# A 2x2x3 block product in 11 products instead of 12 for the last group's hidden layer, and the last x transposed two pieces later

## The chip, the cores and the metric

The kernel runs on one core of a Trainium2 chip. The metric is the device time of one execution in microseconds (us). PE is TensorE, DVE is VectorE, ACT is ScalarE, POOL is GpSimd, SP is SyncE. SBUF is the core's working memory; PSUM is the memory that matmuls write, eight banks of 512 fp32 values per partition. All arithmetic is in fp32.

## The reference

Two blocks follow each other. A delta-rule attention runs over 4 batches of 8 heads, 768 positions and 48 dimensions, and its output, 3072 tokens by 384, goes into a feed-forward layer with three first-layer weights and a maximum:

```python
for t in range(S):
    y[:, :, t] = np.einsum('bhd,bhde->bhe', q[:, :, t], state)
    v_old = np.einsum('bhde,bhd->bhe', state, kt)
    state = state + bt * np.einsum('bhd,bhe->bhde', kt, vt - v_old)
x = y.transpose(0, 2, 1, 3).reshape(3072, 384)
h = np.maximum(np.maximum(x @ w1, x @ w2), x @ w3)      # 3072 x 768
out = h @ w_out                                          # 3072 x 384
```

Here kt is the normalized key. The changed code belongs to `x @ w` for the last 512 tokens.

## The kernel before

The attention is worked in chunks of 64 positions, and the tokens go through the feed-forward layer in `GROUPS` = 6 groups of 512. The order of the instructions is written out by hand. The generator `ffn(m)` yields after each piece of the feed-forward work of group m; the loop at L1319 runs over these pieces, numbered from 0, and after each one issues the links of the attention of the next group that `LINKS` (L1210) names for that piece. So group m's matmuls lie between the attention steps of group m + 1. Within an engine, instructions run in the order in which they are issued.

`hidden(f, lo, w)` (L1050) makes one tile of 128 features of h for 512 tokens, feature-major. `less_first` has replaced w2 and w3 by w2 - w1 and w3 - w1, so that from group 1 on h is max(0, x(w2 - w1), x(w3 - w1)), and x w1 is added after the second layer as x (w1 w_out), whose matrix `both_layers` leaves in `w_sb[0]`. That leaves two weights, `w_sb[1]` and `w_sb[2]`. For each of the six feature tiles and each of the two weights, three matmuls of 128x128 by 128x512 (L1057) sum over the 384 inner values in a tile of `ps_ffn`, which has two buffers. ScalarE writes the first weight's product to h with a Relu (L1067); VectorE takes the maximum with the second's (L1071). This makes 12 pieces.

`outputs(m, hs)` (L947) makes the second layer of the last two groups, also with fewer block products (Winograd's form of Strassen's scheme, with weights that `cross_weights` prepares): 11 pieces of products of 192 columns (L960), with sums on VectorE (L989) and copies on ScalarE (L994, L1011, L1015, L1021). The pieces of group 4 (`GROUPS - 2`) are thus 0 to 11 for the hidden layer and 12 to 22 for the outputs. Group 5, the last, has no attention beside it.

The last x comes to the last group in two halves of 256 tokens: y is written to DRAM (`y_blocks`, L839), read back in another order (`read_y`, link w, L850) and transposed in blocks of 32 by VectorE (`turn_y`, link X, L861). Of group 5's halves, X0 stands after piece 14 of group 4 and X1 after piece 17. In VectorE's queue X1 thus stands behind the three differences issued in piece 17 (`op(s14[j], a12[j], s32[j], minus)`, L1023) and ahead of the sums of pieces 18 to 22.

`ps_two` (L83) gives PSUM tiles of two banks, three of them in turn. `kpad` and `kmore` are SBUF tiles that hold keys while the attention runs; `w_bits` is the tag of five SBUF buffers in which weights and turned keys are staged, and `square` that of 17 buffers for h, among others.

Of the kernel before, what the change touches and what calls it, by code (L numbers as in the profile page):

```python
# [9 lines left out]
FP32 = mybir.dt.float32  # L10
# [4 lines left out]
ALU = mybir.AluOpType  # L15
# [8 lines left out]
def kernel(  # L24
# [31 lines left out]
    nc = tc.nc  # L56
# [5 lines left out]
    KT = DM // 128  # L62
    FT = DFF // 128
    NP = H // 2
    UNITS = NCH * 2
    GROUPS = UNITS // 4
# [5 lines left out]
    work = ctx.enter_context(tc.tile_pool(name="work", bufs=2))  # L72
# [7 lines left out]
    def ps_ffn(shape, name):  # L80
        return psum.tile(shape, FP32, name=name, tag="ffn", bufs=2)

    def ps_two(name):  # L83
        return psum.tile([128, 2, 512], FP32, name=name, tag="two", bufs=3)


    kpad = [const.tile([128, H, DP], FP32, name=f"kpad{i}") for i in range(4)]
    kmore = [const.tile([128, 2, H, DP], FP32, name=f"kmore{i}") for i in range(2)]
# [20 lines left out]
    def rows(bb):  # L109
        return slice(C * bb, C * (bb + 1))  # L110
# [70 lines left out]
    for bb in range(2):  # L181
        nc.gpsimd.affine_select(
            out=mask[rows(bb)], in_=mask[rows(bb)], pattern=[[1, C]], base=-1,
# [4 lines left out]
    t1 = [const.tile([128, 2, H, BL], FP32, name=f"t1{i}") for i in range(NU)]  # L188
# [5 lines left out]
    w_sb = [const.tile([128, KT, DFF], FP32, name=f"w{i}_sb") for i in range(3)]  # L194
# [112 lines left out]
    def square(name):  # L307
        return work.tile([128, H, C], FP32, name=name, tag="square", bufs=17)
# [169 lines left out]
    def blocks(m, queue=nc.sync):  # L478
        if m == 1:
            xs[m] = in_wo(0)  # L480
        else:
            xs[m] = work.tile([128, 2, HB * BL + HB], FP32, name="x_bl", bufs=1)
        queue.dma_start(
            out=in_rows(xs[m]),
            in_=at_d[m].rearrange("c f b h j i -> (c f b h) j i"),
        )
# [232 lines left out]
    xts, rhss, qss, us, yts = {}, {}, {}, {}, {}  # L719
# [184 lines left out]
    PAIRS = FT // 2  # L904
    crossed = {}

    def cross_weights(part):

        left, right = slice(0, HALF), slice(HALF, DM)
        top, bottom = wo_sb[:, 0:PAIRS], wo_sb[:, PAIRS:FT]  # L910
        spare = w_sb[0][:, :, DM : 2 * DM]
        minus = nc.vector.tensor_tensor
        if part == 0:
            minus(
                out=spare[:, :, right], in0=bottom[:, :, right], in1=top[:, :, right],
                op=ALU.subtract,
            )
            minus(
                out=top[:, :, right], in0=top[:, :, right], in1=top[:, :, left],
                op=ALU.subtract,  # L920
            )
            return
        minus(
            out=spare[:, :, left], in0=bottom[:, :, right], in1=top[:, :, right],
            op=ALU.subtract,
        )
        fourth = []
        for n in range(2):
            t = work.tile([128, DM], FP32, name="mant", bufs=2)
            for i in range(2 - n):  # L930
                fourth.append(t[:, HALF * i : HALF * (i + 1)])
        for j in range(PAIRS):
            minus(
                out=fourth[j], in0=wo_sb[:, PAIRS + j, left], in1=spare[:, j, left],
                op=ALU.subtract,
            )
        crossed.update(
            b11=[top[:, j, left] for j in range(PAIRS)],
            b21=[bottom[:, j, left] for j in range(PAIRS)],
            b22=[bottom[:, j, right] for j in range(PAIRS)],  # L940
            t1=[top[:, j, right] for j in range(PAIRS)],
            t2=[spare[:, j, left] for j in range(PAIRS)],
            t3=[spare[:, j, right] for j in range(PAIRS)],
            t4=fourth,
        )

    def outputs(m, hs):  # L947
# [95 lines left out]
        store(m5, 1, 1)  # L1043
        yield

    def ffn(m):
        xt = xts[m]
        hs = {}

        def hidden(f, lo, w):  # L1050
            if f not in hs:
                hs[f] = square("h").rearrange("p h c -> p (h c)")
            h = hs[f][:, lo : lo + w]
            for i in range(m > 0, 3):
                p_h = ps_ffn([128, TOK], "p_h")[:, 0:w]
                for t in range(KT):
                    nc.tensor.matmul(  # L1057
                        p_h,
                        w_sb[i][:, t, f * 128 : (f + 1) * 128],
                        xt[:, t, lo : lo + w],  # L1060
                        start=(t == 0),
                        stop=(t == KT - 1),
                    )
                if i == 0:
                    nc.scalar.copy(h, p_h)
                elif m and i == 1:
                    nc.scalar.activation(  # L1067
                        out=h, in_=p_h, func=mybir.ActivationFunctionType.Relu
                    )
                else:  # L1070
                    nc.vector.tensor_tensor(out=h, in0=h, in1=p_h, op=ALU.max)  # L1071
                yield


        early = FT // 2 if m == 0 else 0
        for lo in (0, TOK // 2):
            for f in range(early):
                yield from hidden(f, lo, TOK // 2)
        for f in range(early, FT):
            yield from hidden(f, 0, TOK)  # L1080
        if m >= GROUPS - 2:
            yield from outputs(m, hs)
            return
        for i in range(4):
            cc, g = divmod(i, 2)
            p_o = ps_ffn([128, DM], "p_o")
            last = slice(i * 128, (i + 1) * 128)
            terms = [(hs[f][:, last], wo_sb[:, f]) for f in range(FT)]
            if m:
                terms += [(xt[:, t, last], w_sb[0][:, t, 0:DM]) for t in range(KT)]  # L1090
            for n, (stays, moves) in enumerate(terms):
                nc.tensor.matmul(  # L1092
                    p_o, stays, moves, start=(n == 0), stop=(n == len(terms) - 1)
                )
                if m and n == 4:
                    yield
            o_sb = work.tile([128, DM], FP32, name="o_sb")
            nc.scalar.copy(o_sb, p_o)  # L1098
            for bb in range(2):
                tok0 = (2 * bb + g) * S + (2 * m + cc) * C  # L1100
                nc.sync.dma_start(out=out[tok0 : tok0 + C, :], in_=o_sb[rows(bb)])
            yield
# [3 lines left out]
    def some(gen, n):  # L1106
        for _ in range(n):
            if next(gen, gen) is gen:
                break
# [74 lines left out]
    for _ in range(2):  # L1184
# [25 lines left out]
    LINKS = {  # L1210
# [3 lines left out]
    }  # L1214
    EARLY_LINKS = {
# [19 lines left out]
        t=turn, K=load_k, L=lambda n: load_blocks(n, nc.sync),  # L1235
# [4 lines left out]
    def links(m, names):  # L1240
        for name in names.split():
            f, i = name[0], int(name[1])
            if f in RECURS and m < GROUPS:
                RECURS[f](2 * m + i)
            elif f in MADE and m + 1 < GROUPS:
                MADE[f](2 * (m + 1) + i)
            elif f in UNIT and m + 1 < GROUPS:
                UNIT[f](4 * (m + 1) + i)
            elif f == "N" and m + 2 < GROUPS:
                load_blocks(4 * (m + 2) + i)  # L1250

    def queries(names):
        for name in names.split():
            f, n = name[0], int(name[1])
            if f not in OF_KEYS:
                links(0, name)
                continue
            OF_KEYS[f](n)
            if f == "T" and n + 3 < 11:
                load_q(n + 3)  # L1260
# [5 lines left out]
    for i, _ in enumerate(ffn(0)):  # L1266
# [15 lines left out]
        queries(FIRST.get(i, ""))  # L1282
        links(1, EARLY_LINKS.get(i, ""))
        if i == 20:
# [34 lines left out]
    for m in range(1, GROUPS):  # L1319
        for i, _ in enumerate(ffn(m)):  # L1320
            if i == 0:
                some(solving, 3)
            if m == 1 and i in (2, 5, 8):
                both_layers(i // 3)
            if m == GROUPS - 2 and i in (8, 9):
                cross_weights(i - 8)
            if m + 2 < GROUPS:
                if i == 6:
                    blocks(m + 2)
                if i == 8:  # L1330
                    solving = solve(m + 2)
            links(m + 1, LINKS.get(i, ""))
            if i > 7:
                some(solving, 3 if i > 8 else 1)
    by_hand.close()
# [28 lines left out]
```

## Time and profile before

| | us |
|---|---|
| median of 3 runs | 517.81 (512.92 to 519.64) |
| profiled execution | 516.06 |
| its span, first to last instruction | 514.3 |
| PE busy | 492.1 (96% of the span) |
| VectorE busy | 324.8 |
| ScalarE busy | 163.3 |
| hidden layer of the last group, first to last matmul | 457.4 to 488.3 |
| outputs of the last group | 488.3 to the end |

In the views of the trace a line gives the start and the length in us, the engine, the line of the kernel, the operation, what is written and read, the shape, how many such instructions are merged (x), and in brackets for how long the engine stood idle before it and whose end released it. PEld is the weight load of TensorE, which may lie beside a matmul. A matmul of fp32 values leaves two records, so the 36 matmuls of the last hidden layer are 72 records. The rows of groups end with the busy time, the mean of one in ns, and the idle time ahead of them. The rows of windows give for each stretch the busy time of PE, PEld, VectorE, ScalarE and GpSimd, then the granted clock of TensorE as a share of full speed, the share of the DMA engines, and GB/s.

### The profile page before, as it was taken

What the parts mean: (1) busy time and instruction counts of PE and PEld (TensorE: products, weight loads), DVE (VectorE), ACT (ScalarE), POOL (GpSimd) and SP (SyncE); (2) the same over time, 40 slices, a digit from 0 to 9 for tenths busy, and PEclk for the clock granted to TensorE, in tenths of its full rate; (3) what the DMA queues carried; (4) which work ended last, traced back from release to release, by engine and by line L of the source; (5) the groups of instructions that cost most, each with busy time, mean ns of one, the idle gap of its engine ahead of it and who ended that gap; (6) DMA issues with size and microseconds to landing.
All of it is one profiled execution on the core that took longest, in us unless ns stands there. A gap on an engine that the chain in (4) does not pass through costs nothing.

```text
span 514.3 us, 18314 instructions
## 1 busy us (share of the span) xinstructions
PE 492.1 (96%) x7956; PEld 322.2 (63%) x7956; DVE 324.8 (63%) x735; ACT 163.3 (32%) x302; POOL 192.2 (37%) x317
## 2 busy tenths in 40 slices
PE   7678989999999999999999999999999999989996
PEld 6567778856565555665555566555655557964496
DVE  5897789868996430898653987636896234331142
ACT  5585655884422242200242101341101412101110
POOL 7444362783491926670575770513030000000000
PEclk9855989999999999999999999999999999999999
DMA  8937869765055925353765454824343202320002
GB/s 110 203 53 216 190 156 147 192 181 121 2 142 133 183 49 125 100 132 95 155 123 129 114 141 115 154 36 97 79 109 85 39 3 64 76 47 0 1 15 47
DMA packets 106303, 53.47 MB, mean 104 GB/s; under 512 B 89712, under 2 KB 99984, under 8 KB 106224
## 3 DMA queue, kind: packets, MB, share of 16 engines
q1 hardware_dynamic: 94640, 31.55, 30.8%
q0 software_dynamic: 9472, 20.37, 16.3%
q8 instruction: 62, 1.02, 0.9%
q10 hardware_dynamic: 2112, 0.39, 0.5%
q14 instruction: 17, 0.14, 0.1%
HBM read 39.17 MB, written 13.11 MB: 102 GB/s over the span
## 4 chain that ended last, share of the span: by engine, by line
PE 77%; DVE 7%; DMA 7%; issue 2%; ACT 2%; SPq 2%; POOL 1%; DVEq 0%; ACTq 0%; POOLq 0%
PE p_h L1057 35%; PE p_o L1092 17%; PE p_o L960 5%; PE p_g L406 3%; PE p_u L759 2%; PE p_m L894 2%; PE p_s L782 2%; PE p_k L731 2%; DMA kmore<-in_k_dram 2%; PE p_q L731 2%; PE p_y L801 2%; PE p_j L714 2%; DMA x_bl<-at_d 1%; DMA qall<-in_q_dram 1%; DMA y_x<-y 1%
## 5 line engine op out<-in xcount | busy, mean ns | idle before, releaser
L1057 PE MATMUL p_h<-xt,w_sb 128*128 128x512 f32 (+1 forms) x522 | 220.1, 566 | 0.7 <-ACT xt L827 0.6
L1057 PEld LDWEIGHTS p_h<-xt,w_sb 128*128 128x128 f32 x522 | 96.7, 194 | 85.7 <-issue 78.5
L1071 DVE TENSOR_TENSOR h<-h,p_h 128x512 f32<-128x512 f32 (+1 forms) x48 | 29.6, 617 | 85.4 <-PE p_h L1057 85.1
L1092 PE MATMUL p_o<-wo_sb,h 128*128 128x384 f32 x192 | 65.3, 490 | 0.0
L552 DVE TENSOR_TENSOR tmp<-x_bl,y_bl 128x31 f32<-128x31 f32 (+20 forms) x139 | 51.4, 370 | 4.1
L556 DVE TENSOR_TENSOR y_bl<-y_bl,tmp 128x31 f32<-128x31 f32 (+20 forms) x139 | 48.5, 349 | 4.8
L1092 PEld LDWEIGHTS p_o<-wo_sb,h 128*128 128x128 f32 x192 | 35.7, 190 | 23.2
L1067 ACT ACTIVATE h<-p_h 128x512 f32<-128x512 f32 x30 | 17.9, 597 | 99.8 <-PE p_h L1057 83.3
L364 POOL DMA_DIRECT2D turned<-in_q_dram x72 | 39.1, 551 | 4.9 <-POOL turned L359 2.9
L1098 ACT COPY o_sb<-p_o 128x384 f32<-128x384 f32 x16 | 7.7, 478 | 85.8 <-PE p_o L1092 79.8
L254 POOL TENSOR_TENSOR w_sb<-mant,up 128x384 int32<-128x384 int32 x18 | 18.8, 1045 | 40.6 <-DVE mant L250 40.5
L406 PEld LDWEIGHTS p_g<-kqt 48*64 48x64 f32 x1216 | 24.0, 138 | 9.4 <-issue 6.4
L406 PE MATMUL p_g<-kqt 48*64 48x64 f32 (+1 forms) x1216 | 27.2, 237 | 1.2 <-ACT kqt L335 1.1
L120 POOL DMA_DIRECT2D kpad<-in_k_dram x32 | 21.8, 690 | 13.8 <-issue 12.7
L789 DVE TENSOR_TENSOR st<-st,p_s 48x768 f32<-48x768 f32 (+1 forms) x18 | 17.1, 950 | 15.4 <-PE p_s L782 15.2
L1092 PE MATMUL p_o<-w_sb,xt 128*128 128x384 f32 x72 | 25.2, 486 | 0.0
L139 POOL DMA_DIRECT2D v_t<-in_v_dram x14 | 11.6, 830 | 35.4 <-PE p_u L759 35.4
L390 DVE TENSOR_TENSOR pt<-p_g,mask 128x512 f32<-128x512 f32 x20 | 13.8, 689 | 16.1 <-PE p_g L406 16.1
L287 POOL TENSOR_TENSOR v_t<-v_t,nrm 128x768 f32<-128x768 f32 x12 | 17.9, 1492 | 9.0 <-DVE nrm L281 8.9
L359 POOL MEMSET turned<- 128x96 f32 x18 | 3.3, 191 | 46.6 <-DVE kqt L380 46.6
L759 PEld LDWEIGHTS p_u<-v_t,ut 64*64 64x64 f32 x768 | 13.3, 141 | 10.3 <-issue 8.4
L1092 PEld LDWEIGHTS p_o<-w_sb,xt 128*128 128x128 f32 x72 | 13.7, 190 | 9.5
(171 smaller groups left out, 731.3 us busy)
## 6 DMA issues: line engine op xcount, KB each, us to landing
out_dram<-o_sb SPq DMA_DIRECT2D x40, 96.0 KB
w_bits<-in_moe_w_dram SPq DMA_DIRECT2D x9, 384.0 KB
w_bits<-in_moe_w_dram POOLq DMA_DIRECT2D x9, 384.0 KB, 5.5
turned<-in_q_dram POOLq DMA_DIRECT2D x72, 48.0 KB, 2.9
kpad<-in_k_dram POOLq DMA_DIRECT2D x32, 96.0 KB, 6.4
y_x<-y SPq DMA_DIRECT2D x16, 192.0 KB
qall<-y_x SPq DMA_DIRECT2D x32, 96.0 KB
v_t<-in_v_dram POOLq DMA_DIRECT2D x14, 192.0 KB, 4.9
```

Of the source, the lines that this page charges most:

```text
L120: queues[bb].dma_start(out=dst[rows(bb ^ g), :, 0:D], in_=src[2 * bb + g, :, c * C : (c + 1) * C, :].rearrange("h p d -> p h d"),)
L254: nc.gpsimd.tensor_tensor(out=dst.bitcast(I32), in0=mant_v.bitcast(I32), in1=up_v, op=ALU.add)
L364: (queue, nc.gpsimd)[i].dma_start(out=t[p0 : p0 + 32, bb, at : at + NP * 2 * D].rearrange("p (j x) -> p j x", j=NP), in_=(k, q)[i][2 * bb ...
L406: nc.tensor.matmul(p_g[rows(bb ^ (g * i)), par, c0 : c0 + C * (1 + whole)], kq[:, 0], kq if whole else kq[:, i],)
L552: nc.vector.tensor_tensor(out=t_v, in0=row.to_broadcast(t_v.shape), in1=column.to_broadcast(t_v.shape), op=ALU.mult,)
L556: nc.vector.tensor_tensor(out=rest, in0=rest, in1=t_v, op=ALU.subtract)
L731: nc.tensor.matmul(p_b[rows(bb), par, c0 : c0 + D], kqt[g][dims(par), j, bb ^ g, i], st[dims(par), bb ^ g, g, j],)
L759: nc.tensor.matmul(p_v[rows(bb ^ g), g, i], ut[c % NU][rows(bb), g, h], rhs[rows(bb), g, h],)
L960: nc.tensor.matmul(to[:, g], a[j][:, 128 * g : 128 * (g + 1)], b[j], start=(start and g == j == 0), stop=(stop and g == 1 and j == PAIRS - 1),
L1057: nc.tensor.matmul(p_h, w_sb[i][:, t, f * 128 : (f + 1) * 128], xt[:, t, lo : lo + w], start=(t == 0), stop=(t == KT - 1),)
L1071: nc.vector.tensor_tensor(out=h, in0=h, in1=p_h, op=ALU.max)
L1092: nc.tensor.matmul(p_o, stays, moves, start=(n == 0), stop=(n == len(terms) - 1))
```

## The change

For the last group alone, `crossed_hidden` takes the place of the six calls of `hidden`. A pair of feature tiles (j and j + 3), the two halves of 256 tokens and the three inner blocks of 128 form, for each weight, a product of 2x3 by 3x2 blocks, plainly 12 block products of 128x128 by 128x256. Winograd's scheme takes 7 for two of the inner blocks, and the third inner block adds 4, so there are 11. They need differences of the weights (`cross_hidden`, issued after pieces 16 and 17 of group 4: four subtractions of 128x384 on VectorE for each weight), sums of the blocks of x (`s1` to `s4`, four operations on VectorE, once), and sums of the products. A unit is one pair with one weight, and there are six. In a unit four tiles of `ps_two` hold two block sums each, one in either bank. ScalarE copies four of the eight sums to `kmore`, VectorE does four additions among copies and four that add the other sums; for the second weight VectorE also takes four maxima with `scalar_tensor_tensor`. Between products the order of the code is that in which each engine works.

The first link of the change, `LAST_LINKS`, moves X1 in group 4 from piece 17 to piece 19, that is, behind the four sums of pieces 18 and 19. Piece 17's other links (K0 to K3) have nothing to do in that group in either kernel.

```diff
+    def cross_hidden(i):
...
+        for to, a, b in ((t3, b22, b12), (b12, b12, b11), (t2, b22, b12), (t4, b21, t2)):
+            nc.vector.tensor_tensor(out=to, in0=a, in1=b, op=ALU.subtract)
...
+    def crossed_hidden(m, hs):
...
+        vec(out=s3, in0=a11, in1=a21, op=ALU.subtract)
+        vec(out=s1, in0=a21, in1=a22, op=ALU.add)
+        vec(out=s2, in0=s1, in1=a11, op=ALU.subtract)
+        vec(out=s4, in0=a12, in1=s2, op=ALU.subtract)
+        for j in range(FT):
+            hs[j] = square("h").rearrange("p h c -> p (h c)")
+        for unit in range(2 * PAIRS):
+            j, i = divmod(unit, 2)
...
+            top, bottom = hs[j], hs[j + PAIRS]
+            held = kmore[unit % 2].rearrange("p a h d -> p (a h d)")
+            m1, m5, m6, m7 = (held[:, 256 * n : 256 * (n + 1)] for n in range(4))
...
+            def times(to, *terms):
+                for n, (stays, moves) in enumerate(terms):
+                    nc.tensor.matmul(
+                        to, w[stays], moves, start=(n == 0), stop=(n == len(terms) - 1)
+                    )
+
+            def result(h, base, p, spare=None):
+                to = h if i == 0 else base if spare is None else spare
+                vec(out=to, in0=base, in1=p, op=ALU.add)
+                if i:
+                    nc.vector.scalar_tensor_tensor(
+                        out=h, in0=h, scalar=0.0, in1=to, op0=ALU.max, op1=ALU.max
+                    )
+
+            def banks(name):
+                t = ps_two(name)
+                return t[:, 0, 0:256], t[:, 1, 0:256]
+
+            p1, p2 = banks("p_1")
+            times(p1, ("b11", a11))
+            nc.scalar.copy(m1, p1)
+            times(p2, ("b21", a12), ("c1", a13))
+            result(top[:, lo], m1, p2, c11)
+            p3, p4 = banks("p_3")
+            times(p3, ("t3", s3))
+            nc.scalar.copy(m7, p3)
+            times(p4, ("t1", s1))
+            nc.scalar.copy(m5, p4)
+            p5, p6 = banks("p_5")
+            times(p5, ("t2", s2))
+            nc.scalar.copy(m6, p5)
+            vec(out=m6, in0=m6, in1=m1, op=ALU.add)
+            vec(out=m7, in0=m7, in1=m6, op=ALU.add)
+            vec(out=m6, in0=m6, in1=m5, op=ALU.add)
+            times(p6, ("c2", a13), ("b22", s4))
+            result(bottom[:, lo], m6, p6)
+            p7, p8 = banks("p_7")
+            vec(out=m5, in0=m5, in1=m7, op=ALU.add)
+            times(p7, ("t4", a22), ("c1", a23))
+            result(top[:, hi], m7, p7)
+            times(p8, ("c2", a23))
+            result(bottom[:, hi], m5, p8)
+            yield
...
+        if m == GROUPS - 1:
+            yield from crossed_hidden(m, hs)
+            early = FT
...
+    LAST_LINKS = {**LINKS, 17: "", 19: "X1"}
...
+            if m == GROUPS - 2 and i in (16, 17):
+                cross_hidden(i - 15)
...
-            links(m + 1, LINKS.get(i, ""))
+            links(m + 1, (LAST_LINKS if m == GROUPS - 2 else LINKS).get(i, ""))
```

More of the change, by code (lines that the diff above doesn't have):

```diff
@@ L1044, in outputs @@
         yield
+    thirds = {}
+    def cross_hidden(i):
+        n = PAIRS * 128
+        w = w_sb[i]
+        b11, b12 = w[:, 0, 0:n], w[:, 0, n : 2 * n]
+        b21, b22 = w[:, 1, 0:n], w[:, 1, n : 2 * n]
+        t = [
+            work.tile([128, 2, n], FP32, name="crossed", tag="w_bits", bufs=5)
+            for _ in range(2)
+        ]
+        t2, t3, t4 = t[0][:, 0], t[0][:, 1], t[1][:, 0]
+        for to, a, b in ((t3, b22, b12), (b12, b12, b11), (t2, b22, b12), (t4, b21, t2)):
+            nc.vector.tensor_tensor(out=to, in0=a, in1=b, op=ALU.subtract)
+        thirds[i] = dict(
+            b11=b11, b21=b21, b22=b22, t1=b12, t2=t2, t3=t3, t4=t4,
+            c1=w[:, 2, 0:n], c2=w[:, 2, n : 2 * n],
+        )
@@ new lines, in crossed_hidden @@
+    def crossed_hidden(m, hs):
+        xt, vec = xts[m], nc.vector.tensor_tensor
+        lo, hi = slice(0, 256), slice(256, 512)
+        a11, a12, a13 = (xt[:, t, lo] for t in range(KT))
+        a21, a22, a23 = (xt[:, t, hi] for t in range(KT))
+        flat = [t.rearrange("p h d -> p (h d)") for t in kpad[0:4]]
+        s1, s2, s3, s4 = (flat[n // 2][:, 256 * (n % 2) :][:, 0:256] for n in range(4))
+        vec(out=s3, in0=a11, in1=a21, op=ALU.subtract)
[6 more added lines that the diff above has]
+            j, i = divmod(unit, 2)
+            w = {
+                name: t[:, 128 * j : 128 * (j + 1)]
+                for name, t in thirds[1 + i].items()
+            }
+            top, bottom = hs[j], hs[j + PAIRS]
+            held = kmore[unit % 2].rearrange("p a h d -> p (a h d)")
+            m1, m5, m6, m7 = (held[:, 256 * n : 256 * (n + 1)] for n in range(4))
+            c11 = flat[2 + unit // 2 % 2][:, 0:256]
+            def times(to, *terms):
[9 more added lines that the diff above has]
+                        out=h, in0=h, scalar=0.0, in1=to, op0=ALU.max, op1=ALU.max
+                    )
+            def banks(name):
[26 more added lines that the diff above has]
+            yield
```

## The prediction

> **What bounds the kernel now.** I read the slices of the page first (PE busy at 9 or more from the tenth slice on), then the chain that ended last, then the timeline from 440 us, where every edited instruction lies. The chain's end:
>
> ```profile
> 451.15 1.23 DVE xt L861
> 455.31 2.22 PE p_o L960 x12
> 457.53 30.90 PE p_h L1057 x72
> 488.43 21.46 PE p_o L960 x132
> ```
>
> From 457.37 us to the last product the end is TensorE, back to back. Before that it is one VectorE queue. The timeline:
>
> ```profile
> 443.42 1.10 DVE L989 TENSOR_TENSOR s<-h,s 128x256 f32<-128x256 f32 x3 [0.52 <-PE p_o L960]
> 449.72 2.11 PE L960 MATMUL p_o<-w_sb,xt 128*128 128x192 f32 x12
> 451.15 1.23 DVE L861 STREAM_TRANSPOSE xt<-qall 128x768 f32<-128x768 f32 x1 [6.63 <-DMA qall<-y_x]
> 451.67 2.11 PE L960 MATMUL p_o<-wo_sb,s 128*128 128x192 f32 x12
> 452.86 0.56 DVE L989 TENSOR_TENSOR o_sb<-o_sb,up 128x384 f32<-128x384 f32 x1
> 453.45 0.56 DVE L989 TENSOR_TENSOR up<-up 128x384 f32<-128x384 f32 x1
> 454.70 0.55 DVE L989 TENSOR_TENSOR o_sb<-o_sb,p_o 128x384 f32<-128x384 f32 x1
> 455.31 2.22 PE L960 MATMUL p_o<-w_sb,xt 128*128 128x192 f32 x12 [1.52 <-DVE o_sb L989]
> 460.14 0.60 ACT L1067 ACTIVATE h<-p_h 128x512 f32<-128x512 f32 x1 [13.58 <-DMA out_dram<-up]
> ```
>
> The transposition of the last x (L861) waits 6.63 us for its DMA at the head of VectorE's queue. Six sums stand behind it, and the product at 455.31 waits for one of them.
>
> Prices of a wait between engines, from the timeline at 44 us and from the groups by shape:
>
> ```profile
> 44.04 0.48 ACT L827 COPY xt<-p_x 128x384 f32<-128x384 f32 x1 [0.16 <-PE p_x L820]
> 44.57 0.50 PEld L1057 LDWEIGHTS p_h<-xt,w_sb 128*128 128x128 f32 x2 [0.97 <-ACT xt L827]
> ...
> L1071 DVE TENSOR_TENSOR h<-h,p_h 128x256 f32<-128x256 f32 x12 | 4.9, 410 | 0.8 <-PE p_h L1057 0.8
> L1065 ACT COPY h<-p_h 128x256 f32<-128x256 f32 x6 | 2.2, 363 | 4.2 <-PE p_h L1057 4.2
> L556 DVE TENSOR_TENSOR y_bl<-y_bl,tmp 128x256 f32<-128x256 f32 x4 | 1.7, 424 | 0.1
> ```
>
> **The Trainium skill.** (1) "Perfetto Trace Analysis", Optimizing Tensor Performance: independent matmul groups should rotate through PSUM banks, so that emptying one overlaps the next group's matmuls. The trace agrees: L1057 alternates two tiles and runs 30.9 us without a gap. (2) "TensorE: Matmul & The Clock Gate", Step-by-step: matmuls stay in program order, only weight loads are pulled ahead. So a waiting matmul holds all behind it, as at 455.31. (3) "VectorE: DVE Perf Modes", The TRN2 errata: an fp32 tensor_tensor takes (N+151)/0.96 ns, 424 at N=256 and 557 at 384. The rows show 424 and 0.56 us. (4) The TensorE page, Part 1: a clock gate halves PE's clock when it is not busy enough; used in a rival below.
>
> **The change, part by part.**
>
> *Products.* 72 matmul records run from 457.37 to 488.26, 30.89 us: 0.429 each at 512 columns, and each fp32 matmul is two records (36 matmuls). At 192 columns 12 records take 1.95 us (449.72 to 451.67), 0.1625 each. On the line between these, 256 columns cost 0.216, and a block product (two records) 0.432. There are 6 units (3 feature pairs, 2 weights) of 11, so 66 x 0.432 = 28.5 us: **-2.4 us** if PE never waits. Weight loads stay beside them (190 ns against 216).
>
> *New waits, the part that decides.* Each unit takes four `ps_two` tiles and puts two block sums, one per bank, in each. The built program of the changed kernel, which shows each instruction's waits without running it, makes the first matmul of the second sum wait until the first sum has been read: p2 waits for ScalarE's copy of p1, p4 for that of p3, p6 for that of p5, and p8 for VectorE's `result` from p7. Each follows at once on the product whose reader it awaits, so nothing covers it. Queued behind are all later products; their readers wait for those.
> A wait on ScalarE: last record's end to the copy's start 0.20 (six records from 457.37 end at 459.94, ACTIVATE starts 460.14); copy 0.363 (L1065); copy's end to PE 0.05 (44.52 to 44.57); the weight load no longer hidden 0.11 (12 records after the wait at 455.31 took until 457.37, 2.06 against 1.95). Sum 0.72 us, three in a unit: 2.16.
> The wait of p8, in us from the unit's start with those waits: p5 ends 4.03, ScalarE's m6 is ready at 4.60; VectorE's three chained sums (0.42 each, 0.03 between) end at 5.95; p6 ends 5.61 and `result` for it ends 6.39; m5's sum then ends about 6.75; p7 ends 6.48. So p7 is read from 6.75 to 7.16 (0.41, L1071), and p8 starts at 7.32: 0.84 late. With the second weight a `scalar_tensor_tensor` (maximum) comes after p6's sum. The trace has none; I take 0.42 like a tensor_tensor of that size (bounds 0.35, its pitch in rows of L989, and 0.55). Then p7 is read until 7.6, and p8 is 1.30 late.
> Two units: 2 x (4.75 + 2.16) + 0.84 + 1.30 = 15.96 us, three times 47.9, in place of 30.9: **+17.0 us**, all of it on the path, as PE alone sets the end here.
>
> *Waits of the next units.* p1 of the next unit reuses a tile that ScalarE has read long before; p5 waits for p8's reader (p8's end + 0.2 + 0.41, or after the running maximum), over 3 us ahead of its need. Free. VectorE's load, 20 operations of about 0.42 = 8.4 us per two units, lies under 16.
>
> *x transposed later.* From piece 17 to 19: VectorE now does the four sums first, and L861 is next to wait. No DMA moves; SP's queue keeps its order, only the stores come earlier. `cross_hidden` adds 8 operations of 128x384 at 0.59 pitch (452.86 to 453.45), 4.7 us, in the 6.63 us that VectorE was idle. Chain: the sums s end 444.5 + 4.7 = 449.2, four sums until 451.6, L861 until 452.8, m7's sum (L989) until 453.4. PE ends its product at 451.67 + 1.95 = 453.62 and need not wait. Its last product starts at 453.62, not 455.31, and the stage ends at 453.62 + 1.95 = 455.57, not 457.37: **-1.8 us**. Without that cover (DMA 0.3 us later) the gain shrinks; bounds 0 and -1.8, I take -1.8.
>
> *Start of the new stage.* Four sums of x wait for m5's sum (ends near 456.2) and need 1.5 us, until 457.7; p3 is due at 455.57 + 2.0. Bound 0 to +0.3; I take 0. *End:* outputs need the first tiles' h at once, done early in the last unit; the six s sums end some 3 us after the last product, 5.85 us after which PE wants them. Free; the last store's 2.6 us stay.
>
> **Sum:** +17.0 - 1.8 = +15.2 us. The profiled execution took 516.06 us (span 514.3): 531.3. It lies 1.75 below the median of the runs, 517.81, which itself spans 512.92 to 519.64. On the median: **533.0**.
>
> **The rivals.**
> *Waits nearly free, products win.* -2.4 - 1.8 = -4.2: 513.6, not slower. It needs each of 24 waits under 4.2/24 = 0.175 us, apart from the gain. Against: the copy alone takes 0.363 and starts after the product. For: only that a hidden way of overlap might exist. 5%.
> *Waits real but short.* If drain and weight load overlap (0.45 per ScalarE wait, 0.6 for p8): 18 x 0.45 + 6 x 0.6 = 11.7, net +7.5: 525.3, within 2% (limit 528.2). For: the ends of matmuls are modelled. 12%.
> *Clock falls.* PE would work 28.5 of 48 us. In windows:
>
> ```profile
> 64.00:68.00 4.00, 2.46 (x71) 2.19 (x71) 3.90 (x9) 2.66 (x6) 1.14 (x3) 0.92 0.38 83
> 68.00:72.00 4.00, 4.00 (x72) 2.98 (x72) 2.92 (x8) 3.07 (x7) 3.60 (x5) 0.65 0.57 119
> 452.00:456.00 4.00, 2.48 (x15) 2.18 (x15) 3.51 (x7) 0.00 (x0) 0.00 (x0) 1.00 0.00 0
> ```
>
> A stretch 62% busy with small matmuls was followed by a clock of 0.65, one as busy with full-size matmuls was not. Half the clock through a third of the stage adds 28.5/3 = 9.5: 542.5. 13%.
> *The change doesn't do what it says.* The order shows 66 products where 36 double-width ones stood, so no.
>
> **Chances.** Waits as computed 70%, the clock 13%, short waits 12%, free waits 5%. Slower by over 2% (about what a measurement of this kernel can tell from no change): 83%; within: 16%; faster: 1%. The range leaves out the free and short waits' lower half and most of the clock case: 526.5 to 541, which also takes in the scatter of the runs and the bounds of the maximum and of x.
>
> **What would show it.** Right: PE's idle time in this stage of some 13 us or more, ended by ScalarE's copies (18 times) and VectorE (6 times); the stage about 48 us; clock 1.00; no PE wait ahead of the last product of the group before. Wrong: PE back to back, a clock under 1, or VectorE never idle there (then its sums, not the shared tiles, are the bound).

## The result, and the profile after

The changed kernel takes 532.0 us (median of 4 runs, 528.93 to 532.52), the kernel before 516.88 us (median of 4, 512.92 to 519.64). The ratio is 1.029, with a 95% interval of 1.0236 to 1.0345: slower, by 15.1 us where +15.2 was predicted. The 532.0 lies inside the forecast range of 526.5 to 541.

The profiled execution took 532.52 us, of which the span is 530.8. The last product of the outputs of group 4 starts at 454.01 us without a wait, the new stage begins at 455.96, and the outputs of the last group begin at 504.69. So the stage took 48.73 us where the 36 double-width products had taken 30.89. What comes after it is as it was: 21.46 us from the first to the last product in the chain, in both kernels.

The timeline of the kernel after around the last x; it answers to the lines from 443 to 455 us of before. In this view and in those that follow, lines that do not bear on the point are left out:

```profile
446.47 0.48 ACT L1021 COPY up<-p_o 128x384 f32<-128x384 f32 x1 [1.48 <-PE p_o L960]
446.47 0.55 DVE L1061 TENSOR_TENSOR crossed<-w_sb 128x384 f32<-128x384 f32 x1
448.71 0.55 DVE L989 TENSOR_TENSOR up<-up,m 128x384 f32<-128x384 f32 x1
450.48 0.56 DVE L989 TENSOR_TENSOR up<-up,o_sb 128x384 f32<-128x384 f32 x1
451.65 1.23 DVE L861 STREAM_TRANSPOSE xt<-qall 128x768 f32<-128x768 f32 x1 [0.62 <-DMA qall<-y_x]
452.06 2.11 PE L960 MATMUL p_o<-wo_sb,s 128*128 128x192 f32 x12
452.80 0.53 DVE L989 TENSOR_TENSOR o_sb<-o_sb,p_o 128x384 f32<-128x384 f32 x1
454.01 2.11 PE L960 MATMUL p_o<-w_sb,xt 128*128 128x192 f32 x12
455.96 0.59 PE L1095 MATMUL p<-xt,w_sb 128*128 128x256 f32 x2
```

VectorE's wait for the DMA has shrunk from 6.63 to 0.62 us: the differences of the weights (L1061) and the four sums (L989) now stand in it. The product at 454.01 has no bracket: the 1.52 us of idle PE are gone.

The same view in the second unit of the new stage (the second weight); L1113, L1118, L1120 and L1123 are ScalarE's copies of p1, p3, p4 and p5:

```profile
464.42 0.37 ACT L1113 COPY kmore<-p 128x256 f32<-128x256 f32 x1 [3.79 <-PE p L1095]
464.85 1.13 PE L1095 MATMUL p<-xt,w_sb 128*128 128x256 f32 x4 [0.46 <-ACT kmore L1113]
466.91 0.70 PE L1095 MATMUL p<-kpad,w_sb 128*128 128x256 f32 x2 [0.51 <-ACT kmore L1118]
468.50 0.70 PE L1095 MATMUL p<-xt,w_sb 128*128 128x256 f32 x2 [0.46 <-ACT kmore L1123]
...
469.40 0.42 DVE L1126 TENSOR_TENSOR kmore<-kmore 128x256 f32<-128x256 f32 x1
469.90 0.59 PE L1095 MATMUL p<-xt,w_sb 128*128 128x256 f32 x2
469.93 0.42 DVE L1101 TENSOR_TENSOR kmore<-kmore,p 128x256 f32<-128x256 f32 x1
470.39 0.43 DVE L1103 SCALAR_TENSOR_TENSOR h<-h,kmore 128x256 f32<-128x256 f32 x1
470.73 0.42 DVE L1130 TENSOR_TENSOR kmore<-kmore 128x256 f32<-128x256 f32 x1
471.25 0.42 DVE L1101 TENSOR_TENSOR kmore<-kmore,p 128x256 f32<-128x256 f32 x1
471.73 1.13 PE L1095 MATMUL p<-xt,w_sb 128*128 128x256 f32 x4 [1.23 <-DVE kmore L1101]
```

Four brackets on PE in one unit: three end with a copy by ScalarE, the fourth with VectorE's sum (L1101 at 471.25) that reads p7. Ahead of that sum stand p6's sum, its maximum (L1103) and m5's sum (L1130). The list of waits, us in all, times and the longest, sums this up for PE over the stage:

```profile
PE p L1095 <- DVE kmore L1101: 3.7, 3, 1.2
...
PE p L1095 <- ACT kmore L1118: 2.9, 6, 0.5
PE p L1095 <- ACT kmore L1113: 2.8, 6, 0.5
PE p L1095 <- ACT kmore L1123: 2.8, 6, 0.5
PE p L1095 <- DVE h L1101: 1.7, 3, 0.6
```

These are 18 waits on ScalarE and 6 on VectorE, with 13.9 us of idle time. The loss, 48.73 - 28.5 = 20.2 us, is larger, because the brackets leave out two parts of each wait. The records of a block product last 0.59 us, although the next product can start 0.43 us after their start, so 0.16 us of lost time counts as busy. And the records after a wait last 0.70 in place of 0.59 us (0.11 more), since the weight load is not hidden there. 24 times 0.27 is 6.5 us, which with 13.9 makes 20.4, the loss but for rounding. The groups by shape give the operation that the trace of before did not have, with 0.425 us:

```profile
L1103 DVE SCALAR_TENSOR_TENSOR h<-h,kmore 128x256 f32<-128x256 f32 x9 | 3.8, 425 | 0.3
```

### The profile page after: what moved, and what is told of

It reads as the page before. It is cut to its first block, busy times and chain, and to the rows that moved or that the text cites. A ratio compares the mean times of both kernels' runs of the same rounds, so it can differ in the third digit from the quotient of the medians.

```text
span 530.8 us, 18547 instructions
## 1 busy us (share of the span) xinstructions
PE 497.7 (94%) x8016; PEld 333.6 (63%) x8016; DVE 350.9 (66%) x801; ACT 168.3 (32%) x320; POOL 192.3 (36%) x317
## 4 chain that ended last, share of the span: by engine, by line
PE 78%; DVE 11%; DMA 4%; ACT 4%; issue 2%; POOL 1%; SPq 0%; DVEq 0%; ACTq 0%; POOLq 0%
PE p_h L1148 28%; PE p_o L1186 16%; PE p_o L960 8%; PE p L1095 4%; PE p_g L406 4%; PE p_u L759 2%; PE p_m L894 2%; PE p_k L731 2%; PE p_s L782 2%; PE p_y L801 2%; PE p_t L329 2%; PE p_q L731 2%; PE p_j L714 1%; DMA x_bl<-at_d 1%; DMA qall<-in_q_dram 1%
## 5 line engine op out<-in xcount | busy, mean ns | idle before, releaser
L1148 PE MATMUL p_h<-xt,w_sb 128*128 128x512 f32 (+1 forms) x450 | 188.2, 560 | 0.7 <-ACT xt L827 0.6
L1148 PEld LDWEIGHTS p_h<-xt,w_sb 128*128 128x128 f32 x450 | 82.6, 194 | 68.8 <-issue 61.8
L1162 DVE TENSOR_TENSOR h<-h,p_h 128x512 f32<-128x512 f32 (+1 forms) x42 | 25.4, 606 | 58.5 <-PE p_h L1148 56.2
L1158 ACT ACTIVATE h<-p_h 128x512 f32<-128x512 f32 x24 | 14.3, 597 | 62.8 <-PE p_h L1148 61.4
L1095 PE MATMUL p<-xt,w_sb 128*128 128x256 f32 x72 | 21.5, 405 | 11.0 <-DVE kmore L1101 3.7
L406 PEld LDWEIGHTS p_g<-kqt 48*64 48x64 f32 x1216 | 25.4, 147 | 9.2 <-issue 6.9
L406 PE MATMUL p_g<-kqt 48*64 48x64 f32 (+1 forms) x1216 | 28.5, 248 | 0.7 <-ACT kqt L335 0.7
L789 DVE TENSOR_TENSOR st<-st,p_s 48x768 f32<-48x768 f32 (+1 forms) x18 | 17.1, 949 | 15.4 <-PE p_s L782 15.2
L1095 PEld LDWEIGHTS p<-xt,w_sb 128*128 128x128 f32 x72 | 12.2, 189 | 19.1 <-ACT kmore L1123 5.2
```

Source lines behind the costliest of these rows:

```text
L406: nc.tensor.matmul(p_g[rows(bb ^ (g * i)), par, c0 : c0 + C * (1 + whole)], kq[:, 0], kq if whole else kq[:, i],)
L1095: nc.tensor.matmul(to, w[stays], moves, start=(n == 0), stop=(n == len(terms) - 1))
L1148: nc.tensor.matmul(p_h, w_sb[i][:, t, f * 128 : (f + 1) * 128], xt[:, t, lo : lo + w], start=(t == 0), stop=(t == KT - 1),)
```

## The experiments

The theory: the time is lost because a unit puts two block sums in each `ps_two` tile, so that the first matmul of the second sum waits until the first sum has been read, with nothing in between to cover it. The profile above gives the waits but not their reason: the tile, not the amount of work, has to be shown as the cause. Rivals: the chains of sums on VectorE and ScalarE set the pace whatever the tiles; the products of 256 columns cost more than half of those of 512.

### A tile for each sum

The products keep their order. The first sum of each two goes to a tile of `ps_ffn`, which is free in this stage and has two buffers, the second to a tile of `ps_two`:

```diff
             def banks(name):
-                t = ps_two(name)
-                return t[:, 0, 0:256], t[:, 1, 0:256]
+                return (
+                    ps_ffn([128, 512], name)[:, 0:256],
+                    ps_two(name + "s")[:, 0, 0:256],
+                )
```

> The changed kernel with each of the eight block sums of a unit in a PSUM tile of its own (the first of each two in a tile of ps_ffn, the second in one of ps_two); products, sums and copies as in the change. Theory 'shared tiles': the 24 waits go (20.2 us of the stage's 48.7), a few tenths come back in the second weight's units, where p7's tile is read late; the stage of L1095 is 28.5 to 30 us, PE idle in it under 2 us, and the time is before - 1.8 - 2.4 + about 0.8, so 513.5 where before is 516.9: faster than before by 0.7%. Rival 'the sums are the bound': the chains of VectorE and ScalarE set the pace whatever the tiles, the stage stays over 40 us and the time over 523.

Measured: 511.75 us (median of 14 runs) beside 516.18 for the kernel before (27 runs), a ratio of 0.9926, interval 0.99 to 0.9952. It beats the kernel before by 0.7%, and the changed one by 20 us. The timeline of this kernel, where a unit of the first weight follows one of the second (L1095 are the products; L1101 is the sum that reads p7 of the unit before):

```profile
473.28 0.59 PE L1095 MATMUL p<-xt,w_sb 128*128 128x256 f32 x2
473.71 1.03 PE L1095 MATMUL p_1s<-xt,w_sb 128*128 128x256 f32 x4
474.49 0.42 DVE L1101 TENSOR_TENSOR kmore<-kmore,p 128x256 f32<-128x256 f32 x1
474.57 0.59 PE L1095 MATMUL p<-kpad,crossed 128*128 128x256 f32 x2
475.00 0.59 PE L1095 MATMUL p_3s<-kpad,w_sb 128*128 128x256 f32 x2
475.44 0.59 PE L1095 MATMUL p<-kpad,crossed 128*128 128x256 f32 x2
475.87 0.59 PE L1095 MATMUL p_5s<-xt,w_sb 128*128 128x256 f32 x2
```

No bracket: PE runs from product to product while ScalarE and VectorE read tiles behind it. The stage lasts from 454.26 to 482.77, 28.51 us, which is 66 x 0.432 to the last digit. VectorE is busy 23.37 us in a window of 29.0 here, so its chains fit. Both rivals fall: the same sums and the same products, in other tiles, take 20.2 us less. The few tenths that I expected back did not come: p7's sum, at 474.49, ends half a microsecond before p5 of the next unit takes its tile at 475.44.

### The last x alone

```diff
-            links(m + 1, LINKS.get(i, ""))
+            links(m + 1, (LAST_LINKS if m == GROUPS - 2 else LINKS).get(i, ""))
```

in the kernel before, with `LAST_LINKS` as in the change.

> The kernel before with only the last x's transposition two pieces later. Theory: the 1.5 us that PE stood idle at 455.3 us is gone, PE's last product of the outputs of group 4 starts 1.7 us earlier, and the time falls by 1.8 us: 515.1 where before is 516.9, a ratio of 0.9965. Rival: the DMA of x ends just as late and the four sums only take its place, the idle time stays and so does the time (0 us).

Measured: 514.17 us beside 516.18, ratio 0.9962, interval 0.9933 to 0.9992. The timeline of this kernel:

```profile
448.74 1.22 DVE L861 STREAM_TRANSPOSE xt<-qall 128x768 f32<-128x768 f32 x1 [2.08 <-DMA qall<-y_x]
449.90 0.50 DVE L989 TENSOR_TENSOR o_sb<-o_sb,p_o 128x384 f32<-128x384 f32 x1
451.36 2.11 PE L960 MATMUL p_o<-w_sb,xt 128*128 128x192 f32 x12
```

The transposition waits 2.08 us instead of 6.63, the sum behind it ends a microsecond before PE needs its tile, and the product at 451.36 does not wait. This half of the change is a gain of 2.0 us (0.4 to 3.5 by the interval), and the products with tiles of their own add 514.17 - 511.75 = 2.4, as 30.89 - 28.51 says.

### The last x back

The changed kernel with `LINKS` in place of `LAST_LINKS` in every group.

> The changed kernel with the last x's transposition back after piece 17. Theory: the four sums wait behind it again, PE stands idle 1.5 us ahead of the last product of group 4's outputs, the time is 1.8 us longer: 533.8 where the change has 532.0. Rival: the eight subtractions that fill VectorE's wait already hide it, 0 us.

Measured: 534.22 us, ratio 1.0362 (1.0321 to 1.0402). In its timeline the four sums stand behind L861 again, and the last product waits:

```profile
449.63 1.24 DVE L861 STREAM_TRANSPOSE xt<-qall 128x768 f32<-128x768 f32 x1 [3.08 <-DMA qall<-y_x]
453.80 2.22 PE L960 MATMUL p_o<-w_sb,xt 128*128 128x192 f32 x12 [1.87 <-DVE o_sb L989]
```

The eight subtractions fill part of VectorE's wait for the DMA (3.08 us are left of 6.63), but the sums still stand behind it, and PE is idle for 1.87 us. The 2.2 us between the medians (534.22 and 532.0) are not all shown to come from this. In the profiled execution the granted clock fell to 0.50 of full speed between 490 and 493 us, within the new stage, which took 50.11 us here in place of 48.73. The row of windows around this, in which the clock is a mean over 16 us:

```profile
484.00:500.00 16.00, 11.88 (x41) 7.81 (x40) 7.53 (x19) 2.35 (x7) 0.00 (x0) 0.89 0.00 1
```

In the same 16 us of the change's profile the clock is 1.00. What x alone costs is better read between two points of the trace, as the section after the experiments does.

### The eighth sum alone in a tile of its own

```diff
-            p7, p8 = banks("p_7")
+            p7, _ = banks("p_7")
+            p8 = ps_ffn([128, 512], "p_8")[:, 0:256]
```

> The changed kernel with the eighth sum alone in a tile of its own (ps_ffn); the first six still share. Theory 'shared tiles': only VectorE's six waits go, 3 x 0.84 + 3 x 1.40 = 6.7 us: 525.3 where the change has 532.0; 18 waits on ScalarE stay, with some 0.46 us of idle PE each. Rival 'the sums are the bound': VectorE takes as long for a unit as before, at most 2 us are gained: 530 to 532.

Measured: 524.78 us, ratio 1.0176 (1.0116 to 1.0236). VectorE's six waits are gone from the list of waits for PE, and the 18 on ScalarE are as they were:

```profile
PE p L1095 <- ACT kmore L1118: 2.9, 6, 0.5
PE p L1095 <- ACT kmore L1113: 2.8, 6, 0.5
PE p L1095 <- ACT kmore L1123: 2.8, 6, 0.5
```

The stage lasts from 456.52 to 498.23, 41.71 us: 7.0 less than in the change. What is left over 28.5, divided by 18, is 0.73 us for a wait on ScalarE.

### The first six in tiles of their own

The other way round: `ps_ffn` and `ps_two` as in the first experiment for p1 to p6, and p7 with p8 in one tile.

```diff
+                if name == "p_7":
+                    t = ps_two(name)
+                    return t[:, 0, 0:256], t[:, 1, 0:256]
```

> The changed kernel with the first six block sums of a unit in tiles of their own, and the seventh and eighth still sharing one. Theory 'shared tiles': the 18 waits on ScalarE go, 18 x 0.73 = 13.1 us, but p6 and p7 then come 0.73 us earlier while VectorE's chain of sums behind p5 does not, so p8's wait grows from 0.84 to about 1.6 and from 1.4 to about 2.1: 13.1 - 6 x 0.73 = 8.7 us less, 523.3 where the change has 532.0. With p8_own's 7.2 that makes 15.9, less than the 20.2 of both together. If the waits simply add, 518.9.

Measured: 526.09 us, ratio 1.0202 (1.0145 to 1.0259), 2.8 above what was expected. The stage itself did as expected, 456.63 to 496.81, 40.18 us, 8.55 less than in the change. Two of p8's six waits in its timeline, one of each weight:

```profile
475.73 1.13 PE L1095 MATMUL p<-xt,w_sb 128*128 128x256 f32 x4 [1.30 <-DVE h L1101]
482.71 1.13 PE L1095 MATMUL p<-xt,w_sb 128*128 128x256 f32 x4 [1.96 <-DVE kmore L1101]
```

They are 0.6 and 1.2 us in the change. With the waits on ScalarE gone PE came earlier to p8, and VectorE's chain, which starts from p5, did not. So the two savings, 7.0 and 8.55 us, do not add up to 20.2: the 18 waits on ScalarE are worth 13.1 us (18 x 0.73), but the one of p6 had hidden 0.7 us of p8's wait in every unit. The profiled execution lost another 1.4 us after the stage, in the outputs (22.84 us in the chain instead of 21.46). There the granted clock fell, as the windows show (the clock is the third number from the end):

```profile
468.00:494.00 26.00, 20.02 (x88) 16.39 (x88) 15.92 (x40) 5.96 (x16) 0.00 (x0) 1.00 0.00 1
494.00:496.00 2.00, 0.05 (x1) 0.00 (x0) 1.72 (x6) 0.00 (x0) 0.00 (x0) 1.00 0.00 0
496.00:500.00 4.00, 3.99 (x13) 3.82 (x14) 3.27 (x9) 0.00 (x0) 0.00 (x0) 0.57 0.00 0
500.00:504.00 4.00, 4.00 (x27) 4.00 (x26) 0.00 (x0) 0.48 (x1) 0.00 (x0) 1.00 0.00 0
```

That is about half of the miss of this execution (526.35 us, where 523.3 was expected). Whether the other runs lost it too, no trace shows; what is left lies within the scatter of this kernel's runs (523.28 to 529.4).

### Each of the three copies twice

```diff
             nc.scalar.copy(m1, p1)
+            nc.scalar.copy(m1, p1)
```

and the same for the copies of p3 and p5.

> The changed kernel with ScalarE's copies from p1, p3 and p5 each done twice in a row (18 more copies of 0.37 us; ScalarE stands idle most of the stage). Theory 'shared tiles': the second sum waits for the second copy too, 0.37 to 0.42 more for each of 18 waits, 6.7 to 7.5 us: 538.7 to 539.5 where the change has 532.0. Rival 'VectorE's sums or the products are the bound': ScalarE has room, no more than 1 us.

Measured: 540.26 us, ratio 1.0492 (1.044 to 1.0545), 8.3 us more than the change and 0.8 above the upper end of what was expected. The stage lasts from 455.06 to 511.05, 55.99 us: 7.26 more, 0.40 for each doubled copy, as expected; the other 1.0 us lies within the scatter of the runs (539.09 to 543.05). ScalarE had room for them, and PE waited for every one. The list of waits, in which L1114, L1120 and L1126 are the second copies:

```profile
PE p L1095 <- ACT kmore L1120: 5.3, 6, 0.9
PE p L1095 <- ACT kmore L1114: 5.2, 6, 0.9
PE p L1095 <- ACT kmore L1126: 5.2, 6, 0.9
```

### Two in a tile, but not neighbours

The tiles still hold two sums, but the pairs are p1 with p3, p2 with p4, p5 with p7, p6 with p8:

```diff
-            p1, p2 = banks("p_1")
+            p1, p3 = banks("p_1")
...
+            p2, p4 = banks("p_2")
             times(p2, ("b21", a12), ("c1", a13))
...
-            p3, p4 = banks("p_3")
...
-            p5, p6 = banks("p_5")
+            p5, p7 = banks("p_5")
...
+            p6, p8 = banks("p_6")
             times(p6, ("c2", a13), ("b22", s4))
...
-            p7, p8 = banks("p_7")
```

> The changed kernel, still two sums in each tile, four tiles in a unit and the products in the same order, but the two sums of a tile are not neighbours any more: p1 with p3, p2 with p4, p5 with p7, p6 with p8, so that another product lies between. Theory 'shared tiles, uncovered': the waits of p3 (0.73 us, under 0.86 of p2) and p7 (0.73 under p6) are covered; p4 waits for VectorE's sum from p2, 0.79 less 0.43 of p3 = 0.36, p8 for its sum from p6, about 0.8; 1.2 us in a unit in place of 3.3: the stage takes 35.5 us and the time is 518.8 where the change has 532.0. Rival 'the sums are the bound' or 'products of 256 columns cost more than the records say': no gain, 530 to 532.

Measured: 520.55 us, ratio 1.0106 (1.0059 to 1.0152). The stage lasts from 453.68 to 491.70, 38.02 us: 10.7 less than in the change, 2.5 more than expected. The waits on ScalarE have left the list; what is left on PE waits for VectorE:

```profile
PE p L1095 <- DVE h L1101: 2.7, 4, 0.8
PE p L1095 <- DVE kmore L1101: 2.3, 5, 0.6
```

Six of these nine are p8's, 0.92 us each with its weight load, where I had 0.8. The first unit's p4 waits 1.1 us in place of 0.36, because the sum that it waits for stands behind the four sums of x. The other five p4 wait 0.4 us each, about as expected; the record of the product before them covers most of that, so they are not in the list. And after the first two units of the second weight p2 waits 0.46 us for p7's reader, which I had not counted. Together 9.6 us, and 28.5 make 38.1. The wait as such is not the harm, then, but a wait without work in front of it. This kernel uses the three `ps_two` tiles of the change and no more, so the gain of the first experiment does not need the two buffers of `ps_ffn` that it added.

## Why the prediction was right, step by step

*Products.* 0.432 us for a block product, 28.5 us for 66: own_tiles, where PE never waits, took 28.51. The gain of 2.4 us is real; it is what the products are worth without the waits.

*Waits on ScalarE.* 0.72 us each was the sum of 0.20, 0.363, 0.05 and 0.11. In the trace p1 ends (0.432 after 455.96) at 456.39, the copy starts at 456.60, lasts 0.37, and PE's weight load starts at 457.02; the four records end 0.11 later than they would after a hidden load. From p8_own it is 0.73. Doubling the copy gave 0.40 more, which is the copy and its start.

*The wait of p8.* For the first weight 0.85 us against 0.84. For the second the term was mis-sized: 1.51 (p7 ends at 470.33, PE restarts at 471.73 and pays 0.11) where I had 1.30. The operation that the trace of before lacked was not at fault, 0.425 us against 0.42. It was the pitch of the sums that wait both for PE and for the VectorE operation ahead of them: p6's sum starts 0.53 us after the operation before it (469.40 to 469.93) and p7's 0.52 (470.73 to 471.25), although PE had ended both products before (p6 at 469.47, p7 at 470.33). I had taken about 0.44 and 0.42. A sum that waits for the operation ahead alone follows at 0.46 (468.94 to 469.40), and one that does not wait for it at 0.33 (462.45 to 462.78, p7's sum of the first weight). In the first weight this shorter pitch made up for the longer one of p6's sum, so 0.85 against 0.84 is partly luck. Three times 0.21 is 0.6 us.

*The sum of the stage.* +17.0 predicted; 48.73 - 30.89 = +17.8 in the profile. The 0.6 above explains most of it.

*The last x.* -1.8 predicted: x_alone gave -2.0, x_back +2.2, the latter with a fallen clock in its profile. The way from ScalarE's copy at L1021 to the first product of the last hidden layer leaves out what differs earlier in an execution, and ends before that clock. In the kernel before it takes 457.37 - 446.08 = 11.29 us, with the copy at

```profile
446.08 0.48 ACT L1021 COPY up<-p_o 128x384 f32<-128x384 f32 x1 [1.48 <-PE p_o L960]
```

In the change it takes 455.96 - 446.47 = 9.49 us, in x_alone 453.31 - 443.81 = 9.50, and in x_back 455.85 - 444.23 = 11.62. So the move is worth 1.8 us in the kernel before, as computed, and 2.1 in the changed one. What was said to be late next, L861, waits 0.62 us for its DMA. It ends at 452.88 and the sum behind it at 453.33, before PE needs that sum at 454.01. The start and the end of the stage cost nothing, as said: p3 started at 457.99, 2.03 us after p1, without a bracket of its own.

*The rivals.* Waits nearly free: no, each copy alone is 0.37 us. Waits real but short: 0.73, not 0.45. The clock: 1.00 through the whole stage of the change, so that rival did not act there. It did act in the profiled executions of x_back and p7_p8_share, and cost 1.4 us in each, where the rival had put 9.5. That the forecast of the time (+15.2 against +15.1) is nearer than its largest term (+17.0 against +17.8) is luck in part: the runs of one kernel scatter by 3 to 7 us.

## What to carry to other kernels

Count a saved product against the hand-offs that come with it: here 2.4 us of matmul time were bought with 24 waits of 0.7 to 1.5 us on the only engine that set the end. Two results in different banks of one tile were one thing to the waits of this program. So a result whose reader is another engine is safer in a tile of its own (28.51 us in place of 48.73), or at least with another product between it and its neighbour in the tile (38.02). Before adding such a stage, read the waits of each matmul in the built program, and ask of each what PE does meanwhile.

## What the runs showed of the hardware

What leaving out a wait saves depends on what stands behind it. The 18 waits on ScalarE cost 0.73 us each, 13.1 in all, but without them the stage was only 8.55 us shorter, because p8's waits for VectorE grew from 0.85 and 1.51 us to 1.58 and 2.23.

A VectorE sum of 128x256 that waits for another engine and for the VectorE operation ahead of it starts 0.52 to 0.53 us after that operation, even when the other engine is done earlier (PE by 0.46 us for p6 and by 0.92 for p7 in the second unit of the change). One that waits for the operation ahead alone starts 0.46 us after it, and one that does not wait for it 0.33.

The Trainium skill, "TensorE: Matmul & The Clock Gate", Why this matters for your kernels, advises against PE-idle gaps of more than about 3 us between bursts. The clock fell here with shorter ones. In p7_p8_share three gaps of 1.96 us occurred in a stage in which PE was busy 77% (20.02 of 26.00 us). After the third the clock was 0.57 of full speed over the next 4 us and cost 1.4 us; after the first two it stayed at 1.00. In x_back no gap within the stage was over 1.23 us, and the clock was 0.89 over 16 us. The traces show it at 0.50 from 497 to 499 us in the first and from 490 to 493 us in the second. At half speed throughout, these means stand for 3.4 and 3.5 us: 4 x 0.43 / 0.5 and 16 x 0.11 / 0.5. The change has the same gaps in this stage, with PE busy 21.45 of 29 us in both from 455 to 484, and kept 1.00, and so did copies_twice with 18.10 of 29. So a gap of 3 us was not needed here, and neither the longest gap nor the busy share decides alone. What does stays open.
